# Funnel attention and mixture of depths: loads half a pair further ahead, weights in eight transfers, gate products per half, interleaved FFN pieces at the end

## The chip, the cores and the metric

The kernel runs on one core of a Trainium2 chip. The metric is the device time of one execution in microseconds (us). The core has a matrix engine (PE, with its weight loads PEld), a vector engine (DVE), a scalar engine (ACT) and GpSimd (POOL), each with its own queue of instructions that is worked off in order; SyncE (SP) issues DMA transfers. Engines wait for each other by semaphores. PSUM, into which PE writes, is handed out here as four buffers of two banks each.

## The reference

The first block is attention with pooled queries: 8 images, 8 heads, 1152 keys, head width 64; neighbouring queries are averaged, so that 576 are left. The second block scores each of the 576 rows (512 wide) of an image with a gate vector, takes the 128 rows with the highest score through a feed-forward network (FFN, 512 to 1024 to 512) and adds the result, weighted by a sigmoid of the score.

```python
q_pool = q.reshape(B, H, S // factor, factor, D).mean(axis=3)
scores = scale * np.matmul(q_pool, k.transpose(0, 1, 3, 2))
scores = scores - np.max(scores, axis=-1, keepdims=True)
attn = np.exp(scores)
attn = attn / (np.sum(attn, axis=-1, keepdims=True) + 1e-09)
attn_out = np.matmul(attn, v).astype(np.float32)
...
x = np.ascontiguousarray(attn_out.transpose(0, 2, 1, 3)).reshape(B, S, H * D)
scores = np.einsum('bsd,d->bs', x, w_gate)
out = x.copy()
for b in range(B):
    top_idx = np.argpartition(-scores[b], capacity)[:capacity]
    xe = x[b, top_idx]
    h = np.maximum(xe @ w1, 0.0)
    ye = h @ w2
    g = 1.0 / (1.0 + np.exp(-scores[b, top_idx]))
    out[b, top_idx] = x[b, top_idx] + g[:, None] * ye
```

## The kernel before

The work is cut into 32 pairs of heads (four to an image, index hp) and each pair into two halves (s = 0, 1) of 288 queries. `run` walks over the 64 halves; half h computes the scores of half h and the weighted values of half h-1. The order in which the code is written is the order in every queue; nothing rearranges it. What a buffer's next user waits for is worked out by the pools from the order of the instructions.

**Scores.** `scores` (L731) makes nine chunks of 128 keys x 2 heads x 288 queries: two matmuls into one PSUM buffer, then one exp on ACT (L738) out of that buffer into the tile p. The pool psum has four buffers, so a chunk's matmuls wait until the exp that read their buffer last has ended. `weighted` (L746) is 18 matmuls on the p of the half before, into one buffer, which ACT copies out (L754).

**Sums.** `folded` adds p up: three POOL adds (L763), two DVE folds (L768) and a small sum (L777). After the second half of a pair `normalized` merges the sums across partitions with one small matmul (L797) into a PSUM tile, DVE adds 1e-9 (L807) and inverts (L815), POOL multiplies the attention output avb by it (x, L816), SP stores x as four pieces of the scratch xs (L824), POOL multiplies x with the gate vector (prod, L829) and DVE adds that up (part, L835).

**Loads.** `load_pair` issues kb and qb (four each, one buffer each) and v_sb (two, three buffers) from SP at the first half of the pair ahead; `prepare_pair` adds neighbouring queries on POOL (qp, L710) and transposes on DVE (kT L713, qT L717). It is called at the second half, so the transposes stand in DVE's queue behind everything that the first half's iteration put there. At the start the qb of the first pair are issued by ACT. w_gate (four transfers, L665), w1 and w2 (one of 2 MB each, L666, L667) are issued by SP in the second iteration, ahead of the loads of the third pair.

**Routing.** `routed` is a generator for one image's gate and FFN; `between` advances it by one step per half during the next image: the row scores summed by a matmul with ones (diag, L868), the scores as columns (L654, five small matmuls into the same PSUM tile as the merge), the rank of each row by comparisons on DVE (cmp L894/L903, tie L913, one row tile per step), sigmoid (L924, L925), a table meta of row numbers (L930, L931, L934), a selection matrix pick (L941), the index matmul (L953, again into the merge's tile), a gather of the chosen rows (xe, L965), their transposes (L980), FFN1 (L991, 64 matmuls), FFN2 (L1003, 16 matmuls) and a scatter (L1018). After the last half the flag `ending` is set and what is left of the last two images' routings is run step by step. `outside` counts sums outside of a range; a second path of the program that a nonzero count would start did not run.

## Time and profile before

| | us |
|---|---|
| median of 3 runs (lowest to highest) | 846.47 (844.48 to 847.41) |
| the profiled execution, its own time | 844.71 |
| its span, first to last instruction | 843.0 |
| PE busy | 767.9 (91%) |
| DVE busy | 510.1 (61%) |
| ACT busy | 371.8 (44%) |
| POOL busy | 410.6 (49%) |

All durations in the following come from the profiled execution, so sums are made against its span of 843.0 us, with 1.7 us around it. A row of the timeline gives start, duration, engine, line, operation, tiles and how many instructions were put together; in brackets stands how long the engine had been idle and what ended that. The granted clock is that of PE: 1.00 is the upper of its two levels, 0.50 the lower. Busy shares are means over a span in which the stages have different limits; a wait is read in its place.

### The profile page before, as it was taken

The numbers are of one execution on the slowest core, as the hardware profiler recorded it, in microseconds if no ns is written. First come the engines' busy times: TensorE is split into PE (matmuls) and PEld (weight loads), VectorE is DVE, ScalarE is ACT, GpSimd is POOL, SyncE is SP. The second block draws the span as 40 slices with busy tenths as digits, with TensorE's granted clock in tenths as the row PEclk, the third lists the DMA queues.
The fourth block names the chain that finished last, engine by engine and source line by source line (L and its number), as shares of the span: only waits on it lengthen the run. The fifth ranks groups of instructions, "written<-read, shape, count | busy, mean of one in ns | idle before, by whom it ended". The sixth has DMA issues, their size and how long they took to land.

```text
span 843.0 us, 13988 instructions
## 1 busy us (share of the span) xinstructions
PE 767.9 (91%) x5503; PEld 515.8 (61%) x5503; DVE 510.1 (61%) x848; ACT 371.8 (44%) x681; POOL 410.6 (49%) x316
## 2 busy tenths in 40 slices
PE   6959999979999799988999899998999989999786
PEld 4646656656756567656666567565675656756464
DVE  4546667875548764586546865378643866457640
ACT  5525655625345343554336443454444554426110
POOL 3545665636346353654526554364634554436400
PEclk9979999989999999998999999998999989999889
DMA  9997785878616587177962586636885667630310
GB/s 143 252 147 113 99 157 96 109 90 153 99 38 102 91 162 100 32 94 106 155 92 50 87 144 112 97 50 97 148 100 83 76 88 141 111 62 15 69 42 29
DMA packets 453547, 84.97 MB, mean 101 GB/s; under 512 B 450656, under 2 KB 450656, under 8 KB 453216
## 3 DMA queue, kind: packets, MB, share of 16 engines
q1 hardware_dynamic: 447456, 79.20, 61.3%
q0 software_dynamic: 1280, 4.20, 1.6%
q10 hardware_dynamic: 4736, 0.59, 0.7%
q8 instruction: 45, 0.74, 0.4%
q14 instruction: 30, 0.25, 0.1%
HBM read 72.42 MB, written 20.97 MB: 111 GB/s over the span
## 4 chain that ended last, share of the span: by engine, by line
PE 55%; DVE 21%; ACT 7%; POOL 7%; DMA 3%; SPq 3%; issue 2%; ACTq 0%; POOLq 0%; DVEq 0%
PE ps L731 22%; PE ps L746 17%; DVE fold L768 9%; PE ps L991 7%; ACT p L738 7%; PE ps L1003 7%; POOL prod L829 3%; DMA qb<-in_q_dram 2%; POOL x L816 2%; DVE tie L913 2%; POOL acc L763 1%; SPq L689 1%; SPq L683 1%; DVE kT L713 1%; DVE gate L925 1%
## 5 line engine op out<-in xcount | busy, mean ns | idle before, releaser
L738 ACT ACTIVATE p<-ps 128x576 f32<-128x576 f32 x576 | 325.3, 678 | 137.9 <-PE ps L731 87.8
L731 PE MATMUL ps<-qT,kT 64*128 64x288 f32 x2304 | 326.2, 434 | 41.3 <-DVE qT L717 36.9
L763 POOL TENSOR_TENSOR acc<-p 128x576 f32<-128x576 f32 x192 | 266.2, 1415 | 162.9 <-ACT p L738 162.8
L731 PEld LDWEIGHTS ps<-qT,kT 64*128 64x128 f32 x2304 | 240.8, 199 | 114.5 <-issue 47.3
L746 PE MATMUL ps<-p,v_sb 128*64 128x288 f32 x2304 | 293.3, 409 | 0.0
L746 PEld LDWEIGHTS ps<-p,v_sb 128*64 128x64 f32 x2304 | 159.9, 137 | 125.6 <-ACT p L738 21.2
L768 DVE TRANSPOSE_TENSOR_REDUCE fold<-p 128x54 f32<-128x1728 f32 x64 | 125.6, 1963 | 141.6 <-ACT p L738 141.6
L768 DVE TRANSPOSE_TENSOR_REDUCE fold<-acc 128x54 f32<-128x1728 f32 x64 | 124.2, 1940 | 11.2 <-POOL acc L763 11.2
L754 ACT COPY av<-ps 128x288 f32<-128x288 f32 x64 | 25.5, 398 | 222.4 <-PE ps L746 218.5
L816 POOL TENSOR_TENSOR x<-avb,rec 128x576 f32<-128x576 f32 x32 | 37.0, 1157 | 131.8 <-DVE rec L815 131.8
L835 DVE TENSOR_REDUCE part<-prod 128x18 f32<-128x576 f32 x32 | 24.1, 753 | 88.0 <-POOL prod L829 88.0
L991 PE MATMUL ps<-xeT,w 128*128 128x128 f32 x512 | 61.4, 282 | 0.8 <-ACT xeT L983 0.7
L991 PEld LDWEIGHTS ps<-xeT,w 128*128 128x128 f32 x512 | 59.9, 197 | 1.2 <-ACT xeT L983 1.1
L1003 PE MATMUL ps<-w,hT 128*128 128x512 f32 x128 | 57.0, 598 | 0.0
L710 POOL TENSOR_TENSOR qp<-qb 128x576 f32<-128x576 f32 (+1 forms) x33 | 45.2, 1370 | 23.5 <-DMA qb<-in_q_dram 23.3
L713 DVE STREAM_TRANSPOSE kT<-kb 128x1152 f32<-128x1152 f32 (+1 forms) x33 | 44.0, 1332 | 14.8 <-DMA kb<-in_k_dram 14.8
L1018 POOL DMA_INDIRECT out_dram<-xe,index x8 | 8.2, 1030 | 82.6 <-DVE xe L1010 82.6
L829 POOL TENSOR_TENSOR prod<-x,w_gate 128x576 f32<-128x576 f32 x32 | 44.9, 1404 | 2.5
L1003 PEld LDWEIGHTS ps<-w,hT 128*128 128x128 f32 x128 | 23.7, 190 | 29.5 <-issue 29.4
L998 ACT ACTIVATE hT<-ps 128x512 f32<-128x512 f32 x16 | 9.6, 597 | 65.6 <-PE ps L991 65.6
L1010 DVE SCALAR_TENSOR_TENSOR xe<-ps,own_gate,xe 128x512 f32<-128x512 f32 x8 | 6.0, 750 | 49.3 <-PE ps L1003 49.3
L913 DVE SCALAR_TENSOR_TENSOR tie<-sc_row,gate_sc,before 128x128 f32<-128x128 f32 (+1 forms) x40 | 32.1, 802 | 0.0
(65 smaller groups left out, 295.4 us busy)
## 6 DMA issues: line engine op xcount, KB each, us to landing
v_sb<-in_v_dram SPq DMA_DIRECT2D x64, 288.0 KB, 5.2
kb<-in_k_dram SPq DMA_DIRECT2D x124, 144.0 KB, 4.6
qb<-in_q_dram SPq DMA_DIRECT2D x124, 144.0 KB, 4.7
xs<-x SPq DMA_DIRECT2D x128, 72.0 KB, 2.3
out_dram<-xs SPq DMA_DIRECT2D x8, 1152.0 KB, 6.0
w<-in_moe_w_dram SPq DMA_DIRECT2D x2, 2048.0 KB, 15.2
kb<-in_k_dram SPq DMA_DIRECT2D x8, 72.0 KB, 3.9
qb<-in_q_dram ACTq DMA_DIRECT2D x8, 72.0 KB, 4.0
```

The source lines that it names most:

```text
L710: nc.gpsimd.tensor_tensor(out=qp[:, qs, :], in0=pair["q"][:, qs, 0, :], in1=pair["q"][:, qs, 1, :], op=ALU.add)
L713: nc.vector.transpose(pair["kT"][:, i * nk * BLK : (i + 1) * nk * BLK], pair["k"][:, ks, :].rearrange("p n d -> p (n d)"),)
L731: nc.tensor.matmul(sc[:, j, 0:n], lhsT=pair["kT"][rows, c * P : (c + 1) * P], rhs=pair["qT"][rows, qs], start=True, stop=True,)
L738: nc.scalar.activation(p[:, c // G, c % G, :, :], sc[:, :, 0:n], AF.Exp, scale=self.scale)
L746: nc.tensor.matmul(av[j * self.D : (j + 1) * self.D, 0:n], lhsT=half["pair"]["v"][:, j, c, :], rhs=half["p"][:, c // G, c % G, j, :], star ...
L763: nc.gpsimd.tensor_tensor(out=acc[:, u, :], in0=units[:, 0, u, :], in1=units[:, 1, u, :], op=ALU.add)
L768: nc.vector.tensor_reduce(fold[:, a, :], of.rearrange("p u (m d) -> p (u m) d", d=BLK), AX.X, ALU.add, apply_transpose=True,)
L816: nc.gpsimd.tensor_tensor(out=x[:, hp, :, :], in0=pair["avb"][:, :, :], in1=rec[:, :].unsqueeze(2).broadcast_to([P, self.QB, BLK]), op=ALU ...
L829: nc.gpsimd.tensor_tensor(out=prod[:, :, :], in0=x[:, hp, :, :], in1=self.w_gate[:, hp : hp + 1, :].broadcast_to([P, self.QB, BLK]), op=AL ...
L913: nc.vector.scalar_tensor_tensor(out=tie[0:rows, 0:rows], in0=sc_row[0:rows, at : at + rows], scalar=own, in1=self.before[0:rows, 0:rows], ...
L991: nc.tensor.matmul(pv[:, f, 0:w], lhsT=self.w1[:, c, (f0 + f) * P : (f0 + f + 1) * P], rhs=xeT[:, c, 0:w], start=(c == 0), stop=(c == self ...
L1003: nc.tensor.matmul(ps[0:w, 0 : self.Dm], lhsT=hT[:, f, 0:w], rhs=self.w2[:, f, :], start=(f == 0), stop=(f == self.NFC - 1),)
```

## The change

- **Loads and transposes.** The loads of pair n+2 are issued at the second half of pair n, half a pair earlier than before, and the transposes of pair n+1 (qp, kT, qT) stand at the end of the first half's iteration, ahead of the merge's sums of the pair that is finished there. The second pair's loads are issued before the loop.
- **Weights.** w_gate is loaded from ACT's queue at the start (four transfers); w1 and w2 are cut into four transfers of 512 KB each, one per half from the third on, behind that half's loads.
- **Gate products.** prod is now the undivided avb times the gate vector, half a pair at a time, on POOL after each half's `drained`; DVE sums it up one half later (red), and one small DVE multiply by rec makes part. The tile x is per pair.
- **Routing.** The table meta is prepared at the start by 16 small POOL operations for all images, so L930 and L931 are gone from the loop; the add of L925 moves to POOL. One of the rank steps is joined to the next, and one empty step is gone. The columns and the index matmul get a PSUM tile of their own instead of the merge's.
- **Ending.** FFN1 and FFN2 yield after each group of matmuls, and an explicit list of pieces mixes image 6's FFN (old) with image 7's routing (new). The count's two DVE operations stand earlier, its matmul just ahead of the last FFN.

The core of the diff:

```diff
+        self.meta = const.tile([P, self.B, self.NT, 3], F32, name="meta")
+        for b in range(self.B):
+            nc.gpsimd.tensor_copy(self.meta[:, b, :, 0], self.token[:, :])
+            nc.gpsimd.tensor_scalar(
+                out=self.meta[:, b, :, 1],
...
-    def load_weights(self):
+    def load_gate(self):
         gate = self.w_gate_in.rearrange("(n j d) -> n j d", n=self.NPAIR, j=2)
         for j, ds, rows in self.quarters():
-            nc.sync.dma_start(self.w_gate[rows, :, :], _rows_of(gate[:, j, ds], BLK))
-        nc.sync.dma_start(self.w1[:, :, :], self.w1_in.rearrange("(c p) f -> p c f", p=P))
-        nc.sync.dma_start(self.w2[:, :, :], self.w2_in.rearrange("(c p) d -> p c d", p=P))
+            self.nc.scalar.dma_start(self.w_gate[rows, :, :], _rows_of(gate[:, j, ds], BLK))
+
+    def weight_loads(self):
...
+        for c in range(self.ND):
+            yield self.nc.sync.dma_start(self.w1[:, c, :], w1[:, c, :])
+        for c in range(0, self.NFC, 2):
+            yield self.nc.sync.dma_start(self.w2[:, c : c + 2, :], w2[:, c : c + 2, :])
...
     def drained(self, half):
...
+        nc.vector.transpose(
+            pair["avb"][:, ns, :].rearrange("p n d -> p (n d)"), half["av"][:, :]
+        )
+        nc.gpsimd.tensor_tensor(
+            out=pair["prod"][:, ns, :],
+            in0=pair["avb"][:, ns, :],
+            in1=self.w_gate[:, hp : hp + 1, :].broadcast_to([P, hb, BLK]),
+            op=ALU.mult,
+        )
+
+    def normalized(self, pair):
...
+        ps = self.banks()[:, 0, :]
         nc.tensor.matmul(
             ps[:, 0 : 4 * hb],
...
-        nc.vector.tensor_reduce(pair["part"][:, hp, :], prod[:, :, :], AX.X, ALU.add)
+    def gated(self, half):
...
+        nc.vector.tensor_reduce(pair["red"][:, ns], pair["prod"][:, ns, :], AX.X, ALU.add)
+        if half["s"] == 1:
+            nc.vector.tensor_tensor(
+                out=pair["part"][:, pair["hp"], :],
+                in0=pair["red"][:, :],
+                in1=pair["rec"][:, :],
+                op=ALU.mult,
+            )
...
-        at_ps = yield
+        yield True
         sc = ffn.tile([P, NT], F32, name="gate_sc")
-        self.columns(sc, sc_row, at_ps[:, 64 : 64 + NT])
+        self.columns(sc, sc_row, self.banks()[:, 0, :])
...
-            if t < NF and not self.ending:
-                yield
+            if t < NF and t != 1:
+                yield True
         nc.scalar.activation(gate[:, :], gate[:, :], AF.Exp, scale=-1.0)
-        nc.vector.tensor_scalar(
+        nc.gpsimd.tensor_scalar(
             out=gate[:, :], in0=gate[:, :], scalar1=1.0, scalar2=None, op0=ALU.add
         )
-
-        meta = ffn.tile([P, NT, 3], F32, name="meta")
-        nc.vector.tensor_copy(meta[:, :, 0], self.token[:, :])
-        nc.vector.tensor_scalar(
-            out=meta[:, :, 1], in0=self.token[:, :], scalar1=float(b * Sp), scalar2=None, op0=ALU.add
-        )
+        meta = self.meta[:, b, :, :]
...
-            if not self.ending:
-                yield
-            at_ps = yield
-            ps = at_ps[:, 72:75]
+            yield True
+            ps = self.banks()[:, 0, 0:3]
...
                 self.scores(half)
+                if h > 1:
+                    self.gated(halves[h - 2])
                 self.folded(half)
...
                 self.weighted(done)
                 self.drained(done)
-                self.between(done["pair"] if done["s"] == 1 else None)
...
+            if h < n_halves and s == 0 and loaded:
+                upcoming = loaded
+                self.prepare_pair(upcoming)
+            if h > 0 and done["s"] == 1:
+                self.normalized(done["pair"])
+            if h < n_halves:
+                self.units()
...
+        pieces(old, 4)
+        pieces(new, 1)
+        pieces(old, 1)
+        pieces(new, 1)
+        pieces(old, self.NFC - 5)
+        pieces(new, 3)
+        pieces(old, self.NFC // 2)
+        pieces(new, 1)
+        low = self.counted()
+        pieces(old, self.NFC)
```

**Order on DVE.** Before, at the end of the iteration that finishes an image's last pair (avb is the attention output, transposed; sums and rec belong to the merge):

```order
L788 STREAM_TRANSPOSE avb<-av 128x288
L807 TENSOR_SCALAR sums<-ps 64x18 x2
L815 RECIPROCAL rec<-sums 128x18
L835 TENSOR_REDUCE part<-prod 128x18
L853 TENSOR_REDUCE line<-part 128x18
L857 TENSOR_TENSOR diag<-line,same 128x576
L713 STREAM_TRANSPOSE kT<-kb 128x1152
L717 STREAM_TRANSPOSE qT<-qp 128x576
L768 TENSOR_REDUCE fold<-p 128x54
```

The same place now:

```order
L807 STREAM_TRANSPOSE avb<-av 128x288
L729 STREAM_TRANSPOSE kT<-kb 128x1152
L733 STREAM_TRANSPOSE qT<-qp 128x576
L832 TENSOR_SCALAR sums<-ps 64x18 x2
L840 RECIPROCAL rec<-sums 128x18
L861 TENSOR_REDUCE red<-prod 128x9
L863 TENSOR_TENSOR part<-red,rec 128x18
L890 TENSOR_REDUCE line<-part 128x18
L894 TENSOR_TENSOR diag<-line,same 128x576
L784 TENSOR_REDUCE fold<-p 128x54
```

The transposes kT and qT have moved from behind part, line and diag (here) or the rank steps (elsewhere) to ahead of the merge's sums; rec, part and the routing come after them.

**Order on PE** in the half that makes the columns of an image's scores (numbers after a name tell buffers' users apart; in brackets the engines that are waited for). Before; the row ahead of these is the merge matmul, which writes ps_1060 too:

```order
L654 MATMUL ps_1060<-ident_75,sc_row_974 128x1 [waits DVE_49]
L654 MATMUL ps_1060<-ident_75,sc_row_974 128x1 x3
L654 MATMUL ps_1060<-ident_75,sc_row_974 64x1
L731 MATMUL ps_1099<-qT_901,kT_900 128x288 [waits Activation_49]
L731 MATMUL ps_1099<-qT_901,kT_900 128x288
L731 MATMUL ps_1103<-qT_901,kT_900 128x288 [waits Activation_49]
L731 MATMUL ps_1103<-qT_901,kT_900 128x288
L731 MATMUL ps_1107<-qT_901,kT_900 128x288 [waits Activation_49]
L731 MATMUL ps_1107<-qT_901,kT_900 128x288
L731 MATMUL ps_1111<-qT_901,kT_900 128x288 [waits Activation_49]
L731 MATMUL ps_1111<-qT_901,kT_900 128x288
L731 MATMUL ps_1115<-qT_901,kT_900 128x288 [waits DVE_49]
```

The same place now, from the merge on:

```order
L822 MATMUL ps_1107<-sum_891,merge_105 128x36 [waits DVE_49,Activation_49]
L664 MATMUL ps_1120<-ident_75,sc_row_1025 128x1 [waits Activation_49]
L664 MATMUL ps_1120<-ident_75,sc_row_1025 128x1 x3
L664 MATMUL ps_1120<-ident_75,sc_row_1025 64x1
L747 MATMUL ps_1152<-qT_918,kT_917 128x288 [waits Activation_49]
L747 MATMUL ps_1152<-qT_918,kT_917 128x288
L747 MATMUL ps_1156<-qT_918,kT_917 128x288 [waits Activation_49]
L747 MATMUL ps_1156<-qT_918,kT_917 128x288
L747 MATMUL ps_1160<-qT_918,kT_917 128x288 [waits Activation_49]
L747 MATMUL ps_1160<-qT_918,kT_917 128x288
L747 MATMUL ps_1164<-qT_918,kT_917 128x288 [waits Activation_49]
L747 MATMUL ps_1164<-qT_918,kT_917 128x288
```

Merge and columns had one tile and have two; before, the fifth chunk of the scores waited for DVE, now every chunk of this half, the five that follow too, waits for an exp on ACT.

**Order on PE at the end**, from the last merge on. Before (w_109 is w1, w_110 is w2, the L953 rows are the index matmuls of images 6 and 7):

```order
L797 MATMUL ps<-sum,merge 128x36
L953 MATMUL ps<-meta,pick 128x3 x5
L868 MATMUL ps<-diag,ones 128x288 x2
L980 MATMUL ps<-ident,xe 128x128 x4
L654 MATMUL ps<-ident,sc_row 128x1 x4
L654 MATMUL ps<-ident,sc_row 64x1
L991 MATMUL ps<-xeT,w_109 128x128 x32
L953 MATMUL ps<-meta,pick 128x3 x5
L1045 MATMUL ps<-low,ones 1x2
L1003 MATMUL ps<-w_110,hT 128x512 x8
```

Now (w_126 is w1, w_127 is w2):

```order
L822 MATMUL ps<-sum,merge 128x36
L1019 MATMUL ps<-xeT,w_126 128x128 x16
L905 MATMUL ps<-diag,ones 128x288 x2
L1019 MATMUL ps<-xeT,w_126 128x128 x4
L664 MATMUL ps<-ident,sc_row 128x1 x4
L664 MATMUL ps<-ident,sc_row 64x1
L1019 MATMUL ps<-xeT,w_126 128x128 x12
L1032 MATMUL ps<-w_127,hT 128x512 x4
L983 MATMUL ps<-meta,pick 128x3 x5
L1032 MATMUL ps<-w_127,hT 128x512 x4
L1008 MATMUL ps<-ident,xe 128x128 x4
L1080 MATMUL ps<-low,ones 1x2
```

The matmuls of image 7's routing (diag, columns, index) stood in a row with waits between them; now FFN matmuls of image 6 stand between them. Image 6's index matmul stood behind the last merge and is now one half earlier.

## Rows read from the trace of the kernel before

**Rows 1.** Waits by line: engine, line, releaser: us in total, times, longest.

```profile
PE ps L731 <- DVE qT L717: 36.9, 10, 8.7
```

**Rows 2.** Timeline of PE over one image's period; four adjacent images look alike.

```profile
482.71 7.48 PE L731 MATMUL ps<-qT,kT 64*128 64x288 f32 x36 [3.97 <-DVE qT L717]
...
496.12 1.25 PE L953 MATMUL ps<-meta,pick 128*128 128x3 f32 x9 [1.08 <-DVE sums L807]
...
500.18 2.70 PE L731 MATMUL ps<-qT,kT 64*128 64x288 f32 x20 [0.54 <-DVE own_gate L963]
...
519.70 0.44 PE L654 MATMUL ps<-ident,sc_row 1*128 1x1 f32 x5 [1.29 <-DVE sums L807]
...
527.41 4.64 PE L731 MATMUL ps<-qT,kT 64*128 64x288 f32 x36
...
585.14 7.22 PE L731 MATMUL ps<-qT,kT 64*128 64x288 f32 x34 [3.97 <-DVE qT L717]
```

**Rows 3.** Busy time by stretch: PE, PEld, DVE, ACT, POOL, PE's granted clock, DMA.

```profile
380.30:385.50 5.20, 5.20 (x22) 4.07 (x24) 4.26 (x4) 2.63 (x5) 0.26 (x1) 0.50 0.99 142
121.00:127.30 6.30, 3.49 (x29) 2.10 (x25) 3.37 (x11) 2.68 (x5) 3.73 (x3) 1.00 1.03 172
```

**Rows 4.** Chain of waits ahead of a late qT: start, us, what.

```profile
370.06 1.41 POOL prod L829
...
374.28 1.30 DVE gate L925
...
375.65 1.29 DVE meta L931
...
379.46 0.67 DVE qT L717
```

**Rows 5.** One line's instructions (L925): ns min/median/max, first and last start.

```profile
L925 DVE TENSOR_SCALAR gate<-gate x8: 159/1372/1374, 169.9 to 807.5; 128x5 f32<-128x5 f32 x8
```

**Rows 6.** Timeline of PE at the start.

```profile
8.57 11.73 PE L731 MATMUL ps<-qT,kT 64*128 64x288 f32 x72 [4.07 <-DVE qT L717]
...
24.99 4.64 PE L731 MATMUL ps<-qT,kT 64*128 64x288 f32 x36 [0.18 <-DVE qT L717]
...
52.27 7.66 PE L731 MATMUL ps<-qT,kT 64*128 64x288 f32 x36 [8.71 <-DVE qT L717]
```

**Rows 7.** Timeline of ACT and SP at the start.

```profile
9.94 0.65 ACT L738 ACTIVATE p<-ps 128x576 f32<-128x576 f32 x1 [1.24 <-PE ps L731]
...
20.75 3.92 SPq L665 DMA_DIRECT2D w_gate<-in_moe_w_gate_dram  x4
...
29.59 6.42 SPq L689 DMA_DIRECT2D qb<-in_q_dram  x1
```

**Rows 8.** Timeline of PE at the end.

```profile
781.40 8.95 PE L746 MATMUL ps<-p,v_sb 128*64 128x288 f32 x72
...
797.10 2.26 PE L868 MATMUL ps<-diag,ones 128*128 128x288 f32 x4 [3.78 <-DVE gate_sc L657]
...
822.28 7.41 PE L991 MATMUL ps<-xeT,w 128*128 128x128 f32 x64 [0.67 <-ACT xeT L983]
829.53 7.03 PE L1003 MATMUL ps<-w,hT 128*128 128x512 f32 x16
```

**Rows 9.** Page: a costliest group (busy us, mean ns); a DMA issue (us to landing).

```profile
L713 DVE STREAM_TRANSPOSE kT<-kb 128x1152 f32<-128x1152 f32 (+1 forms) x33 | 44.0, 1332 | 14.8 <-DMA kb<-in_k_dram 14.8
...
kb<-in_k_dram SPq DMA_DIRECT2D x124, 144.0 KB, 4.6
```

**Rows 10.** Timeline of SP: first and last of a pair's eight loads.

```profile
356.63 0.33 SPq L683 DMA_DIRECT2D kb<-in_k_dram  x1
...
362.68 0.99 SPq L689 DMA_DIRECT2D qb<-in_q_dram  x1
```

**Rows 11.** Timeline, PE and ACT, of a half without a wait.

```profile
757.97 4.64 PE L731 MATMUL ps<-qT,kT 64*128 64x288 f32 x36
758.82 5.00 ACT L738 ACTIVATE p<-ps 128x576 f32<-128x576 f32 x9 [0.68 <-PE ps L731]
```

More of the change, by code (lines that the diff above doesn't have):

```diff
@@ L813, in normalized @@
             )
-        rec = self.small.tile([P, self.QB], F32, name="rec")
+        rec = pair["rec"] = self.small.tile([P, self.QB], F32, name="rec")
         nc.vector.reciprocal(rec[:, :], tot)
+        x = self.work.tile([P, self.QB, BLK], F32, name="x")
         nc.gpsimd.tensor_tensor(
-            out=x[:, hp, :, :],
+            out=x[:, :, :],
             in0=pair["avb"][:, :, :],
@@ L825, in normalized @@
                 pair["xs"][:, d0 + ds.start : d0 + ds.stop].rearrange("(i n) d -> i n d", i=BLK),
-                x[rows, hp, :, :],
+                x[rows, :, :],
             )
-        prod = self.work.tile([P, self.QB, BLK], F32, name="prod")
-        nc.gpsimd.tensor_tensor(
-            out=prod[:, :, :],
-            in0=x[:, hp, :, :],
-            in1=self.w_gate[:, hp : hp + 1, :].broadcast_to([P, self.QB, BLK]),
-            op=ALU.mult,
-        )
-        nc.vector.tensor_reduce(pair["part"][:, hp, :], prod[:, :, :], AX.X, ALU.add)
+    def gated(self, half):
+        nc, pair, hb = self.nc, half["pair"], self.HB
+        if half["s"] == 0:
+            pair["red"] = self.small.tile([P, self.QB], F32, name="red")
+        ns = slice(half["s"] * hb, (half["s"] + 1) * hb)
+        nc.vector.tensor_reduce(pair["red"][:, ns], pair["prod"][:, ns, :], AX.X, ALU.add)
[6 more added lines that the diff above has]
+            )
+            if pair["hp"] == self.NPAIR - 1:
+                unit = self.routed(pair["b"], pair["xs"], pair["part"])
+                next(unit)
+                self.routing.append(unit)
     def banks(self):
@@ L1059, in outside, with units @@
         return count_i
-    def between(self, pair):
-        ps = self.banks()[:, 0, :]
-        if pair:
-            self.normalized(pair, ps)
+    def units(self):
         for unit in self.routing[::-1]:
-            try:
-                unit.send(ps)
-            except StopIteration:
+            if not any(unit):
                 self.routing.remove(unit)
-        if pair and pair["hp"] == self.NPAIR - 1:
-            unit = self.routed(pair["b"], pair["xs"], pair["part"])
-            next(unit)
-            self.routing.append(unit)
     def run(self):
@@ L1082, in run @@
         upcoming = self.load_pair(*pairs[0], parts=2)
+        self.load_gate()
         self.prepare_pair(upcoming, parts=2)
+        loaded = self.load_pair(*pairs[1]) if len(pairs) > 1 else None
+        weights = self.weight_loads()
         for h in range(n_halves + 1):
@@ L1090, in run @@
                     if pair["hp"] == 0:
-                        x = self.work.tile([P, self.NPAIR, self.QB, BLK], F32, name="x")
                         xs = self.dram.tile([self.Sp, self.Dm], F32, name="xs")
                         part = self.ffn.tile([P, self.NPAIR, self.QB], F32, name="part")
-                    pair.update(x=x, xs=xs, part=part)
-                    if following:
-                        upcoming = self.load_pair(*following)
-                elif following:
-                    self.prepare_pair(upcoming)
-                if h == 1:
-                    self.load_weights()
+                    pair.update(xs=xs, part=part)
+                elif n + 2 < len(pairs):
+                    loaded = self.load_pair(*pairs[n + 2])
+                else:
+                    loaded = None
+                if h > 1:
+                    next(weights, None)
                 half = {"pair": pair, "s": s}
@@ L1108, in run, with pieces @@
                 self.drained(done)
-                self.between(done["pair"] if done["s"] == 1 else None)
-        self.ending = True
-        self.count = None
-        while self.routing:
-            self.between(None)
-        if self.count is None:
-            self.count = self.outside()
-        return nc.values_load(self.count[0:1, 0:1])
+            if h < n_halves and s == 0 and loaded:
[5 more added lines that the diff above has]
+                self.units()
+        for _ in weights:
+            pass
+        self.gated(halves[-1])
+        new = self.routing.pop()
+        old = self.routing.pop() if self.routing else iter(())
+        def pieces(unit, n):
+            for _ in range(n):
+                next(unit, None)
+        pieces(old, 4)
[8 more added lines that the diff above has]
+        pieces(old, self.NFC)
+        for unit in self.routing + [old]:
+            for _ in unit:
+                pass
+        pieces(new, 1)
+        count = self.outside(low)
+        for _ in new:
+            pass
+        return nc.values_load(count[0:1, 0:1])
 @with_exitstack
```

46 lines of the change are left out of this document (26 added, 20 removed).

## The prediction

> **What bounds the kernel now.** I read the waits first. PE is the engine that is busy almost throughout, and its largest wait is for the transposed queries: 36.9 us in ten pieces, the longest 8.7 us [rows 1]. Next I looked at where they lie, in PE's timeline of one image [rows 2]. From one late transpose to the next are 102.43 us (585.14 - 482.71). In that period PE waits 3.97 us for qT, 1.08 us ahead of the index matmul, 0.54 us in the scores behind it, and 1.29 us ahead of the columns, the last three for DVE to empty the merge's PSUM tile or the columns'. The scores after the long wait take 7.48 us where 4.64 us is normal, since the granted clock is 0.50 there [rows 3], the lower level, after PE stood still. So 9.72 us of each period (3.97 + 2.84 + 1.08 + 0.54 + 1.29) are stalls; the rest is matmuls in a row.
>
> The chain of waits shows why qT is late [rows 4]. kT and qT of the coming pair stand on DVE behind the whole end of the pair before: prod on POOL 1.41 us, then in the last rank step two adds on 5 elements per partition, 1.30 and 1.29 us, then pick, then the transposes. Such an add takes 0.159 us at its fastest and 1.37 at the median [rows 5]; the slow ones ran while POOL was adding. Two places more: at the start PE waits 8.71 us for the third pair's qT and then runs at 7.66 instead of 4.64 us [rows 6], because that pair's loads stand behind the weights, one single issue taking 6.42 us [rows 7]; at the end PE goes from 790.35 (781.40 + 8.95) to 836.56 (829.53 + 7.03) [rows 8].
>
> **Loads and transposes earlier.** The transposes are now placed nearly a whole half ahead of their use (kT 1.33 us [rows 9], qT 0.67 [rows 4], and between their place in the queue and the first use lies a score half and a weighted half, 9.2 us). Do the loads come in time? In SP's queue they follow the four stores of x. From there eight issues take 7.0 us (356.63 to 363.67) [rows 10], the landing 4.6 us and the transpose 1.33 [rows 9]; with stores, qp and sums the loop from one pair's x to the next is, estimated from these, about 19 to 20 us, against a pair of two halves at 9.2 plus merge, routing and FFN, 24 us on average (97/4). It closes. So the 3.97 us and the slow clock behind it go: 6.81 us per image, seven times. In those places nothing else is late by more than the next wait below.
>
> **The new wait.** What now stands behind kT and qT on DVE are the sums of the merge, and so the merge's PSUM tile is held until those are done. The order of PE shows what that does: merge and columns have two tiles, and in that half all nine chunks wait for an exp, none for DVE. Two of the four buffers are thus out of use, and the same holds where the index matmul has its own tile. With two buffers a chunk waits for the exp of the chunk two before it. Price: an exp begins 0.85 us after its chunk (758.82 - 757.97) [rows 11] and takes 0.65 [rows 7], so two chunks need about 1.55 us instead of 1.03 (twice 4.64/9). Nine chunks take 4 x 1.55 + 0.5 = 6.7 to 6.8 us instead of 4.64: +2.2 us for each of two halves per image. In the other two second halves one buffer is out; with three, exp's own pace (5.00/9 = 0.56 [rows 11]) just shows: +0.3. Lower bound 0, if the buffers come back before they are needed; upper bound 3 us per half, if the exps' reads are delayed too. I take 2.2, since it is worked out from the very two rows that form the loop. Added: 4.4 + 0.6 = 5.0 per image.
>
> **Tiles of their own, gate operations, meta.** The waits of 1.08, 0.54 and 1.29 us ahead of and behind the shared tile go (2.91 per image), since no matmul waits for the merge's sums there. The two adds of 1.3 us leave DVE (one to POOL, one to the start), and prod goes off the chain; these lie beside PE work once the transposes are earlier, so I cost them at nothing of their own. Half-size prod is 0.7 us of POOL's time twice, half of 1.41; covered by scores. If it were not covered, qp behind it would be 0.7 late within the slack above.
>
> **Per image:** 6.81 + 2.91 - 5.0 = 4.7 gained, seven times 33 us; a period of about 97.7.
>
> **Start.** The stall of 8.71 + 3.02 = 11.7 us goes: eight pieces of 512 KB stand each behind a half's loads, and no load waits behind 4 MB. Against it, four loads of w_gate move to ACT, where such issues took 3.92 us on SP [rows 7]; the first exp, at 9.94, comes some 2.4 to 3 us later (ACT had some slack there), most of it taken up by four free buffers. Sixteen small POOL operations lie between the first pair's additions: 0 to 2 us on the second pair, which had 0.18 us of wait [rows 6]. I take 1.0 for both: 10.7 gained, between 8.5 and 11.7.
>
> **End.** Of the 46.2 us from the last weighted product on, two FFNs are 28.9 (2 x 7.41 + 2 x 7.03) [rows 8] and the small matmuls some 5; 12.3 are waits (3.78 ahead of the diagonal matmul alone) and lower clock. Now the first FFN's pieces stand between the routing's steps, so the waits have work in front of them. The comparisons and the gather are the two long steps; I leave 2.3 us for them, between 0 and 5, and take 10 as gained.
>
> **Sum:** 843.0 - 33 - 10.7 - 10 = 789.3 of span, and 1.7 around it 791.0 for the profiled execution. The median of before was 1.8 above its profiled run; I forecast 791, with 780 to 803 as this case's own bounds (7 to 10 us from the buffers' price at 2.9 or 1.5 per half over 14 halves, 2 to 3 each from start and end).
>
> **A rule that speaks against it.** In the stretch 121.0 to 127.3 PE was busy 3.49 of 6.30 us and the granted clock stayed at 1.00 [rows 3]. The Trainium skill, on the page "TensorE: Matmul & The Clock Gate", section "A second HAM failure mode: psum-queue depth-cycling", says that PE idling briefly between groups as it cycles through PSUM made its clock go up and down. Two-buffer halves are of that kind, and by it the clock would fall there; the row speaks for no fall, as these halves are two thirds busy (4.64 of 6.8), more than that stretch.
>
> **Rivals.** (1) The clock falls in the two-buffer halves. If it falls through the scores only, they take 9.3 (twice 4.64) instead of 6.8: 14 x 2.5 = +35, 826 us. If it stays down through the weighted product behind them too, another 4.6: 14 x 7.1 = +99, 890 us, slower than before. It decides the sign from 55/14 = 3.9 us lost per such half. For it: the clock falls in this kernel after a stop of 4 us, and takes a whole score half to return [rows 2, 3]. Against it: the half-busy stretch at 1.00. (2) A wait comes back: POOL's qp stands behind prod, DVE's sums behind qp and the transposes, the stores of x behind those, and the next loads behind the stores. If that loop is longer than a pair, or the gather for the transposes of chosen rows lands late, PE waits for qT or xe once or twice an image. At 3 us per image, without a fallen clock: 7 x 3 = +21, 812 us. For it: the loop is my estimate, of 20 in 24 us; against it: DVE and POOL have idle time. (3) The two-buffer price is not paid, because the chunks run ahead or the exps follow sooner: 14 x 2.2 less, less 5 for the rest, about 757 to 770. Against it: the waits stand in the program. (4) The transposes don't get ahead, because kb and qb have one buffer each and the loads wait as long as before: the gain from qT goes and the price of the buffers stays: -10 at the end, -20 for the tiles of their own (7 x 2.91), +35 for the buffers (7 x 5.0), 851 us. Against it: kb and qb are free once kT and qp are made, which is now earlier too.
>
> **Chances.** Forecast case 0.60 (791); wait comes back 0.14 (812); no price for buffers 0.12 (764); clock down in the scores alone 0.05 (826); clock down beyond them 0.06 (890); transposes not ahead 0.03 (851). The range is 768 to 822: it holds the first case, nearly all of the second, some of the third. A measurement of this kernel can tell about 0.3% from no change; faster by more: 0.60 + 0.14 + 0.12 + 0.05 = 0.91; within: 0.01, a part of the last; slower: 0.08, the rest of it and the clock's second case.
>
> **What would show it.** Right: no wait of PE for qT beyond the start; the waits ahead of columns and index gone; score halves of 6.7 us, two per image, and a period of 97 to 98 us; granted clock 1.00 from 25 us on; the third pair's scores starting at about 43; some 36 us from last weighted product to last matmul. Wrong: 0.50 in a two-buffer half; qT or xe among PE's waits; second halves at 4.6 us; a first exp later than 13 us with PE waiting behind it.

## The result and the profile after

The changed kernel took 804.05 us (median of 4 runs, 803.0 to 804.58) against 845.56 us (844.48 to 847.41) before: a ratio of 0.9505 with a 95% interval of 0.9483 to 0.9528. The forecast was 791 us in a range of 768 to 822. The profiled execution took 803.0 us with a span of 801.3.

PE's waits in the changed kernel, by line (engine, line, releaser: us in total, times, longest):

```profile
PE ps L747 <- ACT p L754: 12.3, 52, 0.3
PE ps L1008 <- DMA xe<-xs,index: 7.3, 7, 1.7
...
PE ps L905 <- DVE diag L894: 3.6, 1, 3.6
PE ps L747 <- DVE qT L733: 3.0, 1, 3.0
PE ps L747 <- DVE sums L832: 2.6, 1, 2.6
```

The 36.9 us of waits for qT [rows 1] are down to the one at the very start. New are many short waits of the scores for an exp, one of about 1 us per image for the gathered rows, one for the first diagonal and one for the sums near the end. The start, PE's timeline:

```profile
7.54 11.40 PE L747 MATMUL ps<-qT,kT 64*128 64x288 f32 x72 [3.04 <-DVE qT L733]
...
23.39 4.63 PE L747 MATMUL ps<-qT,kT 64*128 64x288 f32 x36
...
42.28 4.64 PE L747 MATMUL ps<-qT,kT 64*128 64x288 f32 x36
```

The third pair begins at 42.28 in place of 52.27 [rows 6], without a wait and without slow matmuls. ACT at the start: the four issues of w_gate, and a row of four exps that begins with the first:

```profile
6.58 2.25 ACTq L674 DMA_DIRECT2D w_gate<-in_moe_w_gate_dram  x4
...
10.15 2.30 ACT L754 ACTIVATE p<-ps 128x576 f32<-128x576 f32 x4
```

An image in the middle of the run:

```profile
362.60 0.63 PE L1008 MATMUL ps<-ident,xe 128*128 128x128 f32 x4 [0.98 <-DMA xe<-xs,index]
...
406.74 0.44 PE L664 MATMUL ps<-ident,sc_row 1*128 1x1 f32 x5
407.11 1.24 PE L747 MATMUL ps<-qT,kT 64*128 64x288 f32 x8
408.66 1.30 PE L747 MATMUL ps<-qT,kT 64*128 64x288 f32 x8 [0.32 <-ACT p L754]
...
413.18 0.76 PE L747 MATMUL ps<-qT,kT 64*128 64x288 f32 x4 [0.21 <-ACT p L754]
413.87 4.59 PE L762 MATMUL ps<-p,v_sb 128*64 128x288 f32 x36
...
427.89 5.03 PE L747 MATMUL ps<-qT,kT 64*128 64x288 f32 x36
...
437.36 4.63 PE L747 MATMUL ps<-qT,kT 64*128 64x288 f32 x36
```

The waits of 1.08, 0.54 and 1.29 us [rows 2] are gone. The half behind the columns takes 6.8 us to the end of its last matmul (407.11 to 413.94), with a short stop after every second chunk; halves behind a merge alone take 5.03, the others 4.63 to 4.72. The granted clock, in this half and at the last pair (stretch: us, busy time of PE, PEld, DVE, ACT, POOL, then PE's clock and DMA):

```profile
407.10:414.00 6.90, 5.96 (x40) 2.93 (x40) 5.69 (x16) 4.79 (x9) 4.50 (x4) 1.00 0.00 1
742.00:750.60 8.60, 6.00 (x29) 4.45 (x28) 3.98 (x10) 4.30 (x8) 5.81 (x6) 0.60 0.35 65
```

And the end:

```profile
744.68 6.04 PE L747 MATMUL ps<-qT,kT 64*128 64x288 f32 x28 [2.60 <-DVE sums L832]
...
760.27 0.41 PE L822 MATMUL ps<-sum,merge 128*128 128x36 f32 x2
...
773.90 1.33 PE L983 MATMUL ps<-meta,pick 128*128 128x3 f32 x10 [0.56 <-DVE pick L973]
...
787.86 7.03 PE L1032 MATMUL ps<-w,hT 128*128 128x512 f32 x16
```

The merge matmul of each pair is a good milestone. It starts so many us earlier than before:

| merge of pair | before | after | ahead |
|---|---|---|---|
| 2nd | 64.37 | 51.36 | 13.0 |
| 8th | 187.66 | 177.00 | 10.7 |
| 28th | 699.46 | 665.22 | 34.2 |
| 31st | 776.19 | 739.41 | 36.8 |
| 32nd | 790.93 | 760.27 | 30.7 |
| end of the span | 843.0 | 801.3 | 41.7 |

So 13.0 us come from the start, 23.8 from the images, and 4.9 from the end: 6.1 are lost in the last pair and 11.0 gained behind it.

### The profile page after: what moved, and what is told of

It is laid out like the page before. It is cut to its first block, busy times and chain, and to the rows that moved or that the text cites. A ratio compares the mean times of both kernels' runs of the same rounds, so it can differ in the third digit from the quotient of the medians.

```text
span 801.3 us, 14111 instructions
## 1 busy us (share of the span) xinstructions
PE 760.9 (95%) x5503; PEld 475.7 (59%) x5503; DVE 541.9 (68%) x888; ACT 372.7 (47%) x681; POOL 422.1 (53%) x372
## 4 chain that ended last, share of the span: by engine, by line
PE 39%; POOL 20%; issue 18%; DVE 9%; DMA 7%; ACT 4%; SPq 3%; POOLq 0%; ACTq 0%
PE ps L747 15%; POOL acc L779 13%; PE ps L762 12%; PE ps L1019 5%; PE ps L1032 4%; POOL qp L726 4%; ACT p L754 4%; DMA xe<-xs,index 3%; DVE fold L784 2%; DMA out_dram<-xs 2%; POOL x L842 1%; POOL prod L810 1%; DVE qT L733 1%; DMA v_sb<-in_v_dram 1%; DVE part L863 1%
## 5 line engine op out<-in xcount | busy, mean ns | idle before, releaser
L747 PEld LDWEIGHTS ps<-qT,kT 64*128 64x128 f32 x2304 | 205.1, 188 | 125.8 <-ACT p L754 71.3
L810 POOL TENSOR_TENSOR prod<-avb,w_gate 128x288 f32<-128x288 f32 x64 | 51.0, 796 | 209.8 <-DVE avb L807 194.9
L1019 PE MATMUL ps<-xeT,w 128*128 128x128 f32 x512 | 59.6, 276 | 0.6 <-ACT xeT L1011 0.6
L1019 PEld LDWEIGHTS ps<-xeT,w 128*128 128x128 f32 x512 | 58.0, 192 | 0.8 <-ACT xeT L1011 0.7
L733 DVE STREAM_TRANSPOSE qT<-qp 128x576 f32<-128x576 f32 (+1 forms) x33 | 25.1, 760 | 34.4 <-POOL qp L726 34.4
L861 DVE TENSOR_REDUCE red<-prod 128x9 f32<-128x288 f32 x64 | 28.0, 437 | 11.2 <-POOL prod L810 11.2
```

Source lines behind the costliest of these rows:

```text
L733: nc.vector.transpose(pair["qT"][:, i * nq * BLK : (i + 1) * nq * BLK], qp[:, qs, :].rearrange("p n d -> p (n d)"),)
L747: nc.tensor.matmul(sc[:, j, 0:n], lhsT=pair["kT"][rows, c * P : (c + 1) * P], rhs=pair["qT"][rows, qs], start=True, stop=True,)
L810: nc.gpsimd.tensor_tensor(out=pair["prod"][:, ns, :], in0=pair["avb"][:, ns, :], in1=self.w_gate[:, hp : hp + 1, :].broadcast_to([P, hb, B ...
L1019: nc.tensor.matmul(pv[:, f, 0:w], lhsT=self.w1[:, c, (f0 + f) * P : (f0 + f + 1) * P], rhs=xeT[:, c, 0:w], start=(c == 0), stop=(c == self ...
```

## The experiments

All ratios are against the kernel before, run on the same chip beside each kernel.

| run | us | ratio | 95% |
|---|---|---|---|
| the change | 804.05 | 0.9505 | 0.9483 to 0.9528 |
| sums first | 808.95 | 0.9577 | 0.9553 to 0.9602 |
| not ahead | 778.01 | 0.9214 | 0.9184 to 0.9244 |
| end in steps | 826.94 | 0.9802 | 0.9779 to 0.9825 |
| two transfers | 810.97 | 0.9621 | 0.9591 to 0.9650 |
| weights alone | 834.92 | 0.9876 | 0.9849 to 0.9902 |
| product alone | 839.26 | 0.9935 | 0.9915 to 0.9955 |
| product and gate | 838.59 | 0.9920 | 0.9896 to 0.9945 |
| one tile (not ahead) | 811.47 | 0.9605 | 0.9571 to 0.9638 |
| own tiles alone | 827.30 | 0.9812 | 0.9774 to 0.9849 |
| loads ahead only | 786.87 | 0.9301 | 0.9268 to 0.9334 |
| picks between folds (not ahead) | 761.27 | 0.9004 | 0.8981 to 0.9027 |
| sums first, picks between | 788.75 | 0.9344 | 0.9308 to 0.9380 |

**Is the lead of the transposes worth anything?** The theory of the prediction was that it removes the waits for qT. The edit puts loads and transposes back:

```diff
                     pair.update(xs=xs, part=part)
-                elif n + 2 < len(pairs):
-                    loaded = self.load_pair(*pairs[n + 2])
-                else:
-                    loaded = None
+                    if following:
+                        upcoming = self.load_pair(*following)
+                elif following:
+                    self.prepare_pair(upcoming)
...
-            if h < n_halves and s == 0 and loaded:
-                upcoming = loaded
-                self.prepare_pair(upcoming)
```

> The changed kernel with the loads and transposes where they stood before: loads of a pair at the first half of the pair ahead of it, qp, kT and qT at the start of the second half, behind that pair's sums and the rank steps. All else is as changed. Theory (the lead of the transposes is what removed the six waits of 3.97 us): waits for qT come back six times with the lower clock behind them, +41, against -35 for PSUM buffers that come back early: about 810. Rival (the gate's adds and the product taken out of DVE's chain were enough by themselves): no wait for qT over 1 us, four buffers in all halves, about 768 to 775.

It took 778.01 us, 26 less than the change (25 by the ratios). The rival's sign came, no wait for qT beyond the 2.8 us at the start, at a time 3 us above its range; that the gate's adds and the product are enough by themselves is tried further down, and does not hold. PE's timeline, the half of the columns and that of an index matmul:

```profile
398.27 4.83 PE L747 MATMUL ps<-qT,kT 64*128 64x288 f32 x36
...
344.33 5.35 PE L747 MATMUL ps<-qT,kT 64*128 64x288 f32 x28 [1.61 <-DVE sums L832]
...
439.41 3.74 PE L747 MATMUL ps<-qT,kT 64*128 64x288 f32 x28 [1.61 <-DVE sums L832]
```

The columns' half is down from 6.8 to 4.83: its chunks use all four buffers again. In this run the sums and the columns' copies stand ahead of the transposes; that this is the reason is not shown, and the run on loads or transposes below speaks against it. In the index half PE waits 1.61 us for the sums; behind it the clock fell in four of seven images (0.68 at 344.3 to 349.7) and not in the other three (1.00 at 439.4). That the lead came with a price was forecast; that nothing is lost without it in this kernel was not. The lead alone, on the kernel before, was not run.

**Is the order of sums and transposes the whole price?** Only these two calls are swapped:

```diff
-            if h < n_halves and s == 0 and loaded:
-                upcoming = loaded
-                self.prepare_pair(upcoming)
             if h > 0 and done["s"] == 1:
                 self.normalized(done["pair"])
+            if h < n_halves and s == 0 and loaded:
+                upcoming = loaded
+                self.prepare_pair(upcoming)
```

> The changed kernel with one swap: the merge, its two sums, the reciprocal, x and its stores are written ahead of qp, kT and qT of the next pair, not behind them. The merge's PSUM tile is then free about 2 to 3 us earlier. Theory (the tile is held because the sums stand behind the transposes): the score halves of 6.92 us become 5.0 (three buffers), those of 5.03 become 4.64, 14 x 1.9 + 16 x 0.4 = -33 us, about 771 us, and no wait of PE for qT. Rival (DVE gets to the sums late anyway, since it is behind with folds and rank steps): PE waits for the sums or for qT in place of the exps, 800 us or more.

It took 808.95 us. The theory holds for the halves behind a merge alone, which went from 5.03 to 4.63, and falls for the rest: the columns' halves kept the rhythm of two buffers, and in the index halves PE now waited for the sums. A row of each, the columns' half first:

```profile
410.60 1.30 PE L747 MATMUL ps<-qT,kT 64*128 64x288 f32 x8 [0.31 <-ACT p L754]
...
429.83 4.63 PE L747 MATMUL ps<-qT,kT 64*128 64x288 f32 x36
...
453.94 5.40 PE L747 MATMUL ps<-qT,kT 64*128 64x288 f32 x28 [3.28 <-DVE sums L832]
```

That is worse than two buffers: a tile that is handed back early in the program's order but late in time is a wait, and behind it the clock fell: 5.40 us for 28 matmuls, at a granted clock of 0.68 (3.74 at 1.00 in the run not ahead).

**Loads or transposes?** Loads stay ahead, the transposes go back to the second half:

```diff
                 elif n + 2 < len(pairs):
-                    loaded = self.load_pair(*pairs[n + 2])
...
+                    if loaded:
+                        upcoming = loaded
+                        self.prepare_pair(upcoming)
+                    loaded = self.load_pair(*pairs[n + 2]) if n + 2 < len(pairs) else None
```

> The changed kernel with its loads half a pair ahead as changed, and qp, kT and qT back at the start of the second half, behind the sums and the rank steps: DVE's order is that of the run not ahead, SP's that of the change. Theory (the transposes' place ahead of the sums is what holds the buffers): as the run not ahead, 778 us, within 4. Rival (the earlier loads collide with other transfers, stores of x above all): 790 to 804.

786.87 us: between the two, 17 us better than the change and 9 short of the run not ahead. PE waits for no qT in it beyond the start. From the second image on, its columns' halves have the two-buffer rhythm again, although DVE's order is that of the run not ahead. PE's stops, and on DVE the last of the reads of the merge's and the columns' tiles:

```profile
401.90 0.32 DVE L832 TENSOR_SCALAR sums<-ps 64x18 f32<-64x18 f32 x2
402.66 0.14 DVE L669 COPY gate_sc<-ps 64x1 f32<-64x1 f32 x1
402.85 1.30 PE L747 MATMUL ps<-qT,kT 64*128 64x288 f32 x8 [0.32 <-ACT p L754]
...
407.37 0.76 PE L747 MATMUL ps<-qT,kT 64*128 64x288 f32 x4 [0.21 <-ACT p L754]
```

So neither theory is right. No wait for a load shows, and it is not DVE that holds the buffers: both tiles are read out by 402.80, and yet the chunks alternate between the two other buffers up to the end of the half. The order of the program says the same: in this run the buffers of merge and columns go to the third and fourth chunk of the next half, which then wait for nothing; in the run not ahead they go to the third and fourth chunk of the columns' half itself. The buffers come round as the pool handed them out when the program was built. Why it does so with the loads in the one place and not in the other stays open.

**Do the shorter chains alone do it?** On the kernel before, first the product alone (prod from the undivided output, its sum and the multiply by rec right behind rec), then the gate's two adds off DVE as well:

```diff
-        nc.vector.tensor_reduce(pair["part"][:, hp, :], prod[:, :, :], AX.X, ALU.add)
+        nc.vector.tensor_reduce(red[:, :], pair["prod"][:, :, :], AX.X, ALU.add)
+        nc.vector.tensor_tensor(
+            out=pair["part"][:, hp, :], in0=red[:, :], in1=rec[:, :], op=ALU.mult
+        )
```

> The kernel before with one part of the change: the gate product of the undivided output on POOL after each half, its sum and one multiply by rec on DVE, so that DVE no longer waits 2.75 us for POOL's prod ahead of the rank steps and transposes. Theory (the length of DVE's chain sets the six waits of 3.97 us): they shrink to about 1.4 us; 829 us if the clock still falls behind them (6 x 2.6), 813 if it doesn't (6 x 5.4). Rival (the loads or qp on POOL are what is late): no change, 845.

```diff
-        nc.vector.tensor_scalar(
+        nc.gpsimd.tensor_scalar(
             out=gate[:, :], in0=gate[:, :], scalar1=1.0, scalar2=None, op0=ALU.add
         )
...
+        meta = self.meta[:, b, :, :]
```

> The kernel before with two parts of the change: the gate product as in the run on the product alone, and the two adds on 5 elements off DVE (table meta made at the start, the add of one on POOL). Loads, transposes, weights and ending are as before. Theory (the length of DVE's chain sets the waits): 2.6 + 2.6 us are more than 3.97, so the six waits for qT and the lower clock behind them go, 6 x 6.8 = 41, about 804 us. Rival (the transposes stand too late in the queue whatever is taken out): waits of 2 us or more remain, 820 or more.

839.26 and 838.59 us: both theories fall short. The wait for qT shrinks, and the next one grows. Two rows of the second kernel:

```profile
374.73 4.63 PE L742 MATMUL ps<-qT,kT 64*128 64x288 f32 x36 [1.98 <-DVE qT L728]
...
387.33 2.14 PE L964 MATMUL ps<-meta,pick 128*128 128x3 f32 x9 [3.10 <-DVE sums L825]
```

3.97 + 1.08 us of waits became 1.98 + 3.10. The two add up to the same. PE came to the index matmul sooner, DVE to the sums not: a wait that is shortened in one place is had in the next. That DVE's whole work in this pair is the bound fits these rows, and is argued here, not shown. The gate's adds, 2.6 us in the chain, brought nothing that can be measured by themselves.

**Tiles of their own.** On the kernel before, this part alone:

```diff
-        self.columns(sc, sc_row, at_ps[:, 64 : 64 + NT])
+        self.columns(sc, sc_row, self.banks()[:, 0, :])
...
-            ps = at_ps[:, 72:75]
+            ps = self.banks()[:, 0, 0:3]
```

> The kernel before with one part of the change: columns and index matmul in PSUM tiles of their own. There the sums stand ahead of the transposes, so the merge's tile comes back early. Theory (the matmuls' waits for the sums are pure loss and go): 1.08 + 0.54 + 1.29 us per image, 7 x 2.9 = 20, 825 us. Rival (the waits go to the scores behind, for buffers or for the sums): within 5 us of 845.

827.30 us, as expected, though part of the wait moves to the scores behind the index (1.26 to 1.45 us for own_gate, 0.54 before [rows 2]):

```profile
389.58 2.21 PE L731 MATMUL ps<-qT,kT 64*128 64x288 f32 x16 [1.38 <-DVE own_gate L963]
```

And the reverse, the run not ahead with one tile for the three in the loop:

```diff
-        ps = self.banks()[:, 0, :]
+        ps = self.shared = self.banks()[:, 0, :]
...
-        self.columns(sc, sc_row, self.banks()[:, 0, :])
+        ps = self.banks()[:, 0, :] if self.ending else self.shared
+        self.columns(sc, sc_row, ps[:, 64 : 64 + NT])
...
-            ps = self.banks()[:, 0, 0:3]
+            ps = (self.banks()[:, 0, :] if self.ending else self.shared)[:, 72:75]
```

> The changed kernel with loads and transposes where they stood before (as in the run that put them back), and with columns and index matmul in the merge's PSUM tile, as before, in the loop; the ending is as changed. Theory (tiles of their own are a gain only where the sums come early): the columns wait 1.3 us and the index matmul 3.5 us for the sums in each image, 7 x 4.8 = 34, less 7 x 1.6 for the scores' wait that goes: 800 us. Rival (what the tiles of their own save in waits they lose in buffers): 778, within 4 us.

811.47 us, 33 more than with tiles of their own. There PE waits longer ahead of the index than was expected, and the clock falls each time (the matmuls take 2.14 us where 1.23 is usual):

```profile
453.94 2.14 PE L985 MATMUL ps<-meta,pick 128*128 128x3 f32 x9 [3.88 <-DVE sums L833]
```

PE waits for no qT here beyond the start, but the wait has mostly moved and not gone: 3.97 for qT and 1.08 for the index before, 3.88 for the index here, 1.61 with tiles of their own in the run not ahead.

So the tiles of their own, costed in the prediction at 20 us, are worth 18 alone and 33 with the rest: the largest of the parts that were tried alone (the weights 10, the product and the gate's adds 6).

**The start.** The weights alone on the kernel before (w_gate from ACT, eight transfers behind the loads):

```diff
-                if h == 1:
-                    self.load_weights()
+                if h > 1:
+                    next(weights, None)
```

> The kernel before with one part of the change: w_gate from ACT's queue at the start, w1 and w2 in eight transfers, one per half, each behind that half's loads. Theory (the start's stall comes from the weights ahead of the third pair's loads alone): the wait of 8.71 us and the slow scores behind it go, 845 - 11.7 = about 833 us. Rival (loads a half earlier are needed as well): half of the wait stays, 838 or more.

And on the changed kernel two transfers ahead of the third pair's loads:

```diff
+        yield self.nc.sync.dma_start(self.w1[:, :, :], w1)
+        yield self.nc.sync.dma_start(self.w2[:, :, :], w2)
...
+                    for _ in weights:
+                        pass
                     loaded = self.load_pair(*pairs[n + 2])
```

> The changed kernel with w1 and w2 in one transfer of 2 MB each, both issued ahead of the third pair's loads, at the second half, as before. Theory (cutting the weights removed the start's stall): the third pair's scores wait again 5 to 9 us and run at the lower clock at first, 812 to 816. Rival (the loads half a pair earlier are enough): no wait, 803 to 806.

The first took 834.92 us, and the third pair's scores began at 43.82 without a wait: cutting the weights and putting them behind the loads removes the start's stall by itself, without earlier loads. Which of the two does it was not tried apart. The second took 810.97 us: with two whole transfers ahead of them, earlier loads still leave half of the stall:

```profile
45.45 7.46 PE L745 MATMUL ps<-qT,kT 64*128 64x288 f32 x36 [3.45 <-DVE qT L731]
```

3.45 us and 2.8 of slow matmuls are 6.3 of the 6.9 that were lost.

**The end.** The two routings by whole steps in turn, the count last:

```diff
-        pieces(old, 4)
-        pieces(new, 1)
...
+        while self.routing:
+            self.units()
+        count = self.outside(self.counted())
```

> The changed kernel with the interleaved ending undone: after the last half the two routings advance by whole steps, in turn, as in the loop, and the count comes last. Theory (the pieces cover the routing's waits): the diagonal matmul waits some 4 us again, the index and the gather some 3 to 4 together, the count 1 to 2: about 812. Rival (whole steps cover as well): 804, within 2 us.

826.94 us, 23 more, where 8 were expected. The order is not that of the kernel before, so the 23 us are the price of this order and not what the pieces gained: here image 7's index stands behind a whole FFN2 and the whole ranking. Its waits, and a low clock between them:

```profile
766.75 1.21 PE L905 MATMUL ps<-diag,ones 128*128 128x288 f32 x4 [3.88 <-DVE gate_sc L667]
...
790.10 2.36 PE L983 MATMUL ps<-meta,pick 128*128 128x3 f32 x10 [5.94 <-DVE pick L973]
...
796.58 1.09 PE L1008 MATMUL ps<-ident,xe 128*128 128x128 f32 x4 [4.12 <-DMA xe<-xs,index]
```

**Why are the sums late in the index half?** DVE's timeline of the run not ahead shows the five picks at 4.28 us, while POOL adds (429.41 to 433.54), and the sums behind them:

```profile
429.73 4.28 DVE L973 TENSOR_SCALAR pick<-slot_f,rank 128x128 f32<-128x128 f32 x5
...
438.90 0.36 DVE L832 TENSOR_SCALAR sums<-ps 64x18 f32<-64x18 f32 x2
```

Put between DVE's two folds of the next half, they start at 425.29, when POOL's adds have ended (at 425.00):

```diff
             nc.vector.tensor_reduce(
                 fold[:, a, :],
...
+            if a == 0 and self.choose:
+                self.choose()
```

> The run not ahead with one more edit: the five picks, 4.28 us beside POOL's adds, stand between DVE's two folds of the next half in place of ahead of both, where POOL is done or nearly done with its adds. Theory (the picks are slow because POOL runs): they take 1.1 to 2 us there, the sums of that half come 1 to 3 us earlier, PE's seven waits of 1.6 us for the sums go and the clock stays up behind them: 778 - 7 x 2 = about 764 us. Rival (the second fold waits for POOL anyway, DVE ends at the same time): 778, within 3.

761.27 us, and this beats both kernels: 0.9004 of before (0.8981 to 0.9027). DVE and PE there:

```profile
425.29 1.02 DVE L980 TENSOR_SCALAR pick<-slot_f,rank 128x128 f32<-128x128 f32 x5
...
429.49 3.67 PE L749 MATMUL ps<-qT,kT 64*128 64x288 f32 x28 [0.24 <-DVE sums L836]
```

Of the 17 us against the run not ahead, 9.6 are the shorter waits of the seven index halves (1.61 to 0.24) and 7.4 the four halves in which the clock had fallen; here it stayed up in all seven.

The same edit on the run with the sums first:

> The run with the sums first (loads and transposes ahead as changed, the merge's sums ahead of the transposes) and the five picks between DVE's two folds. Theory (there the scores waited 3.28 us for sums that were late because the picks ran slowly beside POOL's adds): the picks take about 1.1 us, the sums come 3 us earlier, the seven waits and the lower clock behind them go, 809 - 7 x 5 = about 774; the halves behind the columns keep two buffers. Rival (the sums were late because DVE has too much to do in that pair, whatever the picks take): waits of over 1.5 us stay, 795 or more.

788.75 us, between theory and rival: the picks take 2.25 us, for POOL's adds still run beside them up to 440.38, and the wait falls from 3.28 to 1.40:

```profile
439.00 2.25 DVE L980 TENSOR_SCALAR pick<-slot_f,rank 128x128 f32<-128x128 f32 x5
...
444.43 3.88 PE L749 MATMUL ps<-qT,kT 64*128 64x288 f32 x28 [1.40 <-DVE sums L836]
```

So the slow picks were more than half of the wait there. How much of the 1.40 us left is DVE's load is not shown, since the picks are still 1.2 us slower than at their 1.02.

## Why the prediction was right, and where it was not

**What bounds the kernel, and what the lead does.** The stalls were read in the right places, and those for qT, the columns and the index went. But the step "So the 3.97 us and the slow clock behind it go" gives the transposes' place as the reason, and the runs don't bear that out: without the lead these waits are gone too, and the lead costs 25 to 26 us on the whole. Nor is it the two shorter chains alone: with these only, the wait moves to the index matmul. Nor is it the tiles of their own: with these alone the waits for qT stay (38.1 us in ten pieces), and with one tile and no lead qT is not waited for either. What the runs show is that the tiles bring 18 to 33 us, since index and columns no longer wait for sums that are late. Which of the smaller moves (red one half later, two rank steps in one) took away the last 2 us of the wait was not tried apart, and stays open, as does what the lead does alone.

**The new wait.** Right in size, and only half right in mechanism. The size: 6.8 us per two-buffer half (6.7 to 6.8 forecast), 5.03 for three buffers (4.94), waits for exps and none for DVE in the columns' halves. The step that failed is "the merge's PSUM tile is held until those are done", as the reason why two buffers are out of use. In the changed kernel DVE reads the two tiles out by 411.85, in the middle of the half (407.11 to 413.94), and no chunk behind that gets their buffers:

```profile
410.95 0.32 DVE L832 TENSOR_SCALAR sums<-ps 64x18 f32<-64x18 f32 x2
...
411.71 0.14 DVE L669 COPY gate_sc<-ps 64x1 f32<-64x1 f32 x1
```

With the sums ahead of the transposes the columns' halves kept the rhythm, in the run with the sums first and in that with only the loads ahead, where both tiles are read out 2.2 us after the merge began. So it is the order in which the pool hands out buffers that sets this price; DVE's order alone does not. For the halves behind a merge alone the reason holds: with the sums first they went to 4.63.

**Per image.** 4.7 us were forecast, and the 20 merges from the 8th to the 28th bring 23.6 us over five periods, 4.7 each. That the two agree to a tenth is partly luck, as about 1 us per image for the gathered rows was not in the sum. The term that failed is "seven times": the trace of before has a wait near 3.97 us for qT six times (176, 279, 380, 483, 585 and 688 us), not seven, and the first image's routing brought a wait of its own, 3.60 us of PE for the diagonal, which stands on DVE behind the transposes and has no FFN ahead of it yet. Between the 2nd and the 8th merge 2.3 us were lost. So the images gave 23.8 us and not 33. The four waits of before that stand in no row yet, and the first diagonal of the changed kernel with the scores behind it:

```profile
175.95 7.26 PE L731 MATMUL ps<-qT,kT 64*128 64x288 f32 x36 [3.98 <-DVE qT L717]
279.00 6.33 PE L731 MATMUL ps<-qT,kT 64*128 64x288 f32 x36 [3.97 <-DVE qT L717]
380.27 7.50 PE L731 MATMUL ps<-qT,kT 64*128 64x288 f32 x36 [3.98 <-DVE qT L717]
687.56 7.46 PE L731 MATMUL ps<-qT,kT 64*128 64x288 f32 x36 [3.97 <-DVE qT L717]
```

```profile
102.64 1.21 PE L905 MATMUL ps<-diag,ones 128*128 128x288 f32 x4 [3.60 <-DVE diag L894]
103.78 4.64 PE L747 MATMUL ps<-qT,kT 64*128 64x288 f32 x36
```

**The start.** 10.7 forecast, 13.0 measured. The 1.0 us set aside for w_gate on ACT and the meta operations was not lost: the four issues took 2.25 us there, not 3.92 [rows 7], the first exp began at 10.15 (9.94 before), and the first scores at 7.54, earlier than 8.57 [rows 6].

**The end.** Behind the last merge 11.0 us were gained, 10 forecast. But behind the index matmul that moved into the last pair the scores waited 2.60 us for late sums, with the granted clock at 0.60 over the stretch; that pair lost 6.1. The prediction had costed this half like the other thirteen: it has four buffers, and so meets the sums. The end's gain was put 5.1 too high and the images' 9.2, the start's 2.3 too low: 12.0 together, which is the span of 801.3 against 789.3.

**The rivals.** The clock stayed at 1.00 in all thirteen two-buffer halves, with PE busy 5.96 of 6.90 us: the row of before was the better guide. By the rule of the Trainium skill ("TensorE: Matmul & The Clock Gate", "A second HAM failure mode: psum-queue depth-cycling") it would have gone up and down there; no run here shows that for these halves. The rival of a returning wait came true in its smallest form, 0.9 to 1.7 us for the gathered rows in six images and 0.45 at the end (7.3 in all). The 851 us of rival (4) leave the start's gain of 10.7 out of the sum without a reason; with it they would be about 840.

## What to carry to other kernels

Removing the largest wait in the list gains little if the engine that it waits for is full in that stretch: look at what the same engine owes next, since that is where the time comes back. Where buffers come from a pool, look in the program as built at which buffer each user gets: a buffer that has been read out helps nobody until the pool hands it on. And multiply a period's gain by the number of rows that show it, not by the number of stages.

## What was not expected of the hardware

Some small DVE instructions are slowed by POOL's beside them: five picks of 128 x 128 took 4.28 us beside POOL's three adds (4.13 us) and 1.02 when POOL stood idle, and one multiply on 18 elements per partition took 0.18 to 2.9 us, the longest beside POOL's adds. The folds kept their 1.9 to 2.0 us either way. The Trainium skill ("SBUF — State Buffer", "SBUF: two separate sides") says that DVE and GpSimd share a pair of ports: a DVE instruction in a two-port mode, or one with two SBUF inputs beside a GpSimd instruction that reads SBUF, and the GpSimd instruction exclude each other, and the one that starts first holds the pair until it ends. These rows agree, but for the 2.9 us, which are longer than one of the adds (about 1.4 us). Moving five such instructions by some 4 us was worth 17 us of the kernel (778.01 to 761.27), since a late sum held a PSUM buffer and the clock fell behind some of the waits. After waits of 1.6 us the granted clock fell in four images and not in three; after the 3.88 us ahead of the index it fell each time; after the 3.60 us ahead of the first diagonal of the changed kernel it stayed at 1.00 (the scores behind it took 4.64 us).
